# K and V of a fused linear-attention and SwiGLU kernel: plain products replaced by two-by-two block products with seven multiplications

## The chip, the cores and the metric

The kernel runs on one core of a Trainium2 chip. The metric is the device time of one execution in microseconds (us). The core has five engines with their own instruction streams: PE (TensorE, the matrix multiplier; its weight loads are listed as PEld), DVE (VectorE), ACT (ScalarE), POOL (GpSimd) and SP (SyncE, which only issues DMA transfers here). They meet through semaphores. Matmul results land in PSUM, eight banks of 128 x 512 fp32; everything else lives in SBUF.

## The reference

```python
xn = _layernorm(x)                       # x: 1 x 2048 x 1024, bf16
# attention block, 32 heads of 32
q, k, v = split(xn @ wqkv)               # wqkv: 1024 x 3072
phi = lambda t: where(t > 0, t + 1, exp(t)) + 1e-6
kv  = einsum("bhsd,bhse->bhde", phi(k), v)
z   = einsum("bhsd->bhd", phi(k))
o   = (phi(q) @ kv) / (phi(q) . z + 1e-6)
s   = o @ wo
# gated feed-forward block
g   = silu((silu(xn @ w_gate) * (xn @ w_up)) @ w_down)   # 1024 -> 3584 -> 1024
out = x + s * g
```

The attention is linear: `kv` and `z` sum over all 2048 tokens before any query is used. So K and V of all tokens come first.

## The kernel before

**Stages.** The 2048 tokens are 16 tiles of 128. The first stage normalises each tile (`ln_tile`), transposes it so that features lie on partitions (`t_tile`), multiplies it with the K and V columns of `wqkv` (`p_piece`), and adds its contribution to `kv` and `z` (`a_tile`). Then, for each half of the tokens (p = 0, 1), the kernel computes Q, gate and up in pairs of weight blocks, normalises Q by the denominators, and runs the down projection together with the attention output (`d_set`), which is joined with `kv` and `wo` into one matrix.

**K and V, lines 530 to 550.** Per tile there are four pieces (c = 0, 1 are K, c = 2, 3 are V), each eight matmuls of 128 x 128 by 128 x 512 into one PSUM bank. `phi_evac` (line 509) takes a K piece out: an exp on ACT, a minimum-and-add on DVE (L515), and a maximum-and-add on DVE (L516) that reads the bank again. A V piece is copied by ACT into `vext`, which has a column of ones per group for `z`. `a_tile` is eight matmuls of 129 columns into three banks (`kvb`) that stay open for the whole stage.

**Layer norm, lines 457 to 471.** DVE computes two `bn_stats` (L462, L463), an aggregate (L464) and variance plus epsilon (L465); POOL raises it to the power -0.5 (L466); DVE subtracts the mean and multiplies (L470).

**Transposes, lines 482 to 495.** Tiles 0 to 3 are transposed by PE into bank 7 (`MISC`), which is kept out of the pool of seven banks, and copied out by ACT. Tiles 4 to 15 use DMA transposes on SP.

**Seven products.** The later stages already use a two-by-two block scheme with seven products instead of eight. Class `Set` (line 636) holds one such product of 128-token or 128-column blocks: `step(m)` issues product m, which is four matmuls. Products 1 and 2 add up in bank a; bank b starts as an ACT copy of product 1 and takes 6, 7 and 4; product 5 is copied by ACT to SBUF (`s5`); DVE adds `s5` to b after step 6 (into bank c, which takes product 3) and again after step 7. The core of it:

```python
elif m == 6:
    self.grp(6, self.b, False)
    self.c = balloc()
    tt([bank_r[self.b], self.s5.r], [bank_r[self.c]], ps[self.c][:, :], ps[self.b][:, :],
       self.s5.ap(F32), ALU.add)
elif m == 7:
    self.grp(7, self.b, False)
```

The products need sums of blocks of both operands. `combos` (line 424) makes T1 to T4 of the moving operand in four DVE instructions, of which T1 overwrites R01; the stationary operand gets four sums too (`wload`, line 697). `run_pair` runs two sets interleaved in the order `PAIRSEQ`, in which steps 6 and 7 of a set are two steps apart.

**What sets the order.** Nothing is issued in the order it is written. `Plan` records each operation with its reads and writes, gives it a deadline (`dl`) from PE's accumulated time, and places operations greedily by a model of each engine's cost (lines 87 to 164). PE may take any ready group among the next six that are not done (`WINDOW=6`); DVE, ACT, POOL and SP take the ready operation with the earliest deadline. DMA loads are held back until 12 us before their deadline (`LEAD`). Each engine then runs its list strictly in order. `urgent` moves a deadline ahead. Banks are handed out by `balloc` and `bfree`, first in, first out, in program order.

Of the kernel before, what the change touches and what calls it, by code (L numbers as in the profile page):

```python
# [14 lines left out]
KB = 1024  # L15
# [204 lines left out]
def build_kernel(nc, A_x, A_wqkv, A_wo, B_w_gate, B_w_up, B_w_down, out, WINDOW=6, NWARM=14, LEAD=12.0):  # L220
# [12 lines left out]
    with ExitStack() as es:  # L233
# [38 lines left out]
        rstd = sbt("rstd", [128, 4, 1], F32)  # L272
        neg_half = sbt("neg_half", [128, 1], F32)
# [9 lines left out]
        MISC = 7  # L283
        banks = deque(range(7))
# [117 lines left out]
        pk_ring = Ring(W, 44 * KB, 2 * KB, 2)  # L402
# [36 lines left out]
        WK0 = 36 * KB  # L439
        wkv_r = [H.reg(WK0 + c * 8 * KB, 8 * KB) for c in range(4)]  # L440
        wkv = [H.at(WK0 + c * 8 * KB, 8 * KB).rearrange("p (kt n) -> p kt n", n=512) for c in range(4)]
        wo_r = [H.reg(68 * KB + c * 8 * KB, 8 * KB) for c in range(2)]
        wo = [H.at(68 * KB + c * 8 * KB, 8 * KB).rearrange("p (g n) -> p g n", n=512) for c in range(2)]

        xslot = {}

        def x_load(i):
            s = x_ring.take()
            xslot[i] = s
            dma([], [s.r], s.ap(), xf[i * 128:(i + 1) * 128, :], dsem("x%d" % s.k), 256 * KB).urgent = 10.0  # L450

        def wkv_load(c):
            dma([], [wkv_r[c]], wkv[c], wqkv_v[:, :, 1024 + c * 512:1024 + (c + 1) * 512], dsem("wkv%d" % c), 1024 * KB)

        xnslot = {}

        def ln_tile(i):
            j = i % 4
            s = xslot[i]
            xa = s.ap()  # L460
            sA, sB, mvr, ver, rsr = named("sA", j), named("sB", j), named("mv", j), named("ve", j), named("rs", j)
            dve([s.r], [sA], lambda h: h.bn_stats(stats[:, j, 0, :], xa[:, 0:512]), 512)  # L462
            dve([s.r], [sB], lambda h: h.bn_stats(stats[:, j, 1, :], xa[:, 512:1024]), 512)  # L463
            dve([sA, sB], [mvr], lambda h: h.bn_aggr(mv[:, j, :], stats[:, j, :, :]), 60)  # L464
            dve([mvr], [ver], lambda h: h.tensor_scalar(veps[:, j, :], mv[:, j, 1:2], EPS_LN, None, ALU.add), 60)  # L465
            pool([ver, nh_r], [rsr], lambda h: h.tensor_tensor(rstd[:, j, :], veps[:, j, :], neg_half[:, :], ALU.pow), 0.56)  # L466
            o = xn_ring.take()
            xnslot[i] = o
            oa = o.ap(FP16)
            dve([s.r, mvr, rsr], [o.r], lambda h: h.tensor_scalar(  # L470
                oa, xa, mv[:, j, 0:1], rstd[:, j, :], ALU.subtract, ALU.mult), 1024, 2.6)

        def xt_dest(i):
            p, j, m = i // 8, (i // 4) % 2, i % 4
            ar = X if p == 0 else P
            return ar, j, m

        def xt_keys(i, k):
            ar, j, m = xt_dest(i)
            return named("xt", i, k)  # L480

        def t_tile(i):
            s = xnslot[i]
            xa = s.ap(FP16)
            ar, j, m = xt_dest(i)
            if i >= 4:
                dst = ar.at(j * 8 * KB, 8 * KB, FP16).rearrange("p (k t) -> p k t", t=512)[:, :, m * 128:(m + 1) * 128]
                PL.op("sp", [s.r], [xt_r(i)], lambda h: h.dma_start_transpose(dst, xa), 0.08, sem=dsem("tx%d" % (i % 2)),
                      nbytes=400 * KB)
                return  # L490
            pb = ps[MISC][:, :].bitcast(FP16).rearrange("p (k t) -> p k t", t=128)
            trs = [(pb[:, kt, :], xa[:, kt * 128:(kt + 1) * 128], ident[:, :]) for kt in range(KT)]
            pe_tr([s.r, ident_r], [bank_r[MISC]], trs)
            dst = ar.at(j * 8 * KB, 8 * KB, FP16).rearrange("p (k t) -> p k t", t=512)[:, :, m * 128:(m + 1) * 128]
            act([bank_r[MISC]], [xt_r(i)], dst, pb[:, :, :], ACT.Identity)

        def xt_r(i):
            ar, j, m = xt_dest(i)
            keys = []
            for kt in range(KT):  # L500
                o = j * 8 * KB + kt * 1024 + m * 256
                keys += ar.reg(o, 256).keys
            return Region(keys)

        def xt_ap(i, kt):
            ar, j, m = xt_dest(i)
            return ar.at(j * 8 * KB + kt * 1024 + m * 256, 256, FP16)

        def phi_evac(src, src_r, out_ap, out_r, kind="ps"):
            e = e_ring.take()  # L510
            ea = e.ap(FP16)
            act([src_r], [e.r], ea, src, ACT.Exp, kind)
            b = B_ring.take()
            ba = b.ap(FP16)
            dve([e.r], [b.r], lambda h: h.tensor_scalar(ba, ea, 1.0, EPS_PHI, ALU.min, ALU.add), 512, 2.6)  # L515
            dve([src_r, b.r], [out_r], lambda h: h.scalar_tensor_tensor(  # L516
                out_ap, src, 0.0, ba, ALU.max, ALU.add), 512)

        kvb = [balloc(), balloc(), balloc()]

        def kv_ap(g):
            return ps[kvb[g // 3]][:, (g % 3) * 129:(g % 3) * 129 + 129]

        vext = TM.at(18 * KB, 4160).rearrange("p (s g n) -> p s g n", s=2, n=130)
        vx_r = [TM.reg(18 * KB, 2080), TM.reg(18 * KB + 2080, 2080)]
        pkv = {}
        for s2 in range(2):
            pool([], [named("vx1", s2), vx_r[s2], pool_chain], lambda h, s2=s2: h.memset(vext[:, s2, :, 128:129], 1.0))

        def p_piece(i, c):  # L530
            b = balloc()
            mms = [(ps[b][:, :], xt_ap(i, kt), wkv[c][:, kt, :], kt == 0, kt == KT - 1) for kt in range(KT)]
            pe_mm([xt_r(i), wkv_r[c]], [bank_r[b]], mms)
            if c < 2:
                if c == 0:
                    pkv[i] = pk_ring.take()
                s = pkv[i].sub(c * 1024, 1024)
                phi_evac(ps[b][:, :], bank_r[b], s.ap(), s.r)
            else:
                hb = c - 2  # L540
                act([bank_r[b], vx_r[i % 2]], [named("vx", i % 2, hb)], vext[:, i % 2, 4 * hb:4 * hb + 4, 0:128],
                    ps[b][:, :].rearrange("p (g n) -> p g n", n=128), ACT.Identity)
            bfree(b)

        def a_tile(i):
            s2 = i % 2
            pk = pkv[i].ap()
            mms = [(kv_ap(g), pk[:, g * 128:(g + 1) * 128], vext[:, s2, g, 0:129], i == 0 and g % 3 == 0, i == NT - 1)
                   for g in range(NG)]
            pe_mm([pkv[i].r, named("vx", s2, 0), named("vx", s2, 1), named("vx1", s2), vx_r[s2]], [bank_r[b] for b in kvb], mms)  # L550

        x_load(0)
        wkv_load(0)
        x_load(1)
        wkv_load(1)
        x_load(2)
        wkv_load(2)
        wkv_load(3)
        x_load(3)
        ln_tile(0)  # L560
        t_tile(0)
        ln_tile(1)
        p_piece(0, 0)
        t_tile(1)
        p_piece(0, 1)
        p_piece(1, 0)
        x_load(4)
        ln_tile(2)
        p_piece(0, 2)
        p_piece(1, 1)  # L570
        t_tile(2)
        p_piece(0, 3)
        p_piece(1, 2)
        a_tile(0)
        ln_tile(3)
        x_load(5)
        p_piece(1, 3)
        for it in range(3, NT + 2):
            if it + 3 < NT:
                x_load(it + 3)  # L580
            if it + 1 < NT:
                ln_tile(it + 1)
            if it < NT:
                t_tile(it)
            if it <= NT:
                for c in range(4):
                    p_piece(it - 1, c)
                a_tile(it - 2)
            else:
                a_tile(it - 2)  # L590


        KVZ = H.at(32 * KB, 2 * KB, FP16).rearrange("p (g n) -> p g n", n=128)
        KVT = H.at(34 * KB, 2 * KB, FP16).rearrange("p (g n) -> p g n", n=128)
        KVZ_r, KVT_r = H.reg(32 * KB, 2 * KB), H.reg(34 * KB, 2 * KB)
        z_r, zi_r, Zb_r = named("z"), named("zi"), named("Zb")
        for q, kb in enumerate(kvb):
            n = 3 if q < 2 else 2
            src = ps[kb][:, 0:129 * n].rearrange("p (g n) -> p g n", n=129)[:, :, 128:129]
            dst = zc[:, 3 * q:3 * q + n].rearrange("p (g n) -> p g n", n=1)  # L600
            dve([bank_r[kb]], [z_r], lambda h, dst=dst, src=src: h.tensor_copy(dst, src), 8)  # L601
# [527 lines left out]
```

## Time and profile before

| what | value |
|---|---|
| median of 3 runs | 764.66 us (762.93 to 766.51) |
| the profiled execution | 765.06 us |
| its span, first to last instruction | 763.1 us |
| PE busy | 748.0 us, 98% |
| DVE busy | 517.6 us, 68% |
| ACT busy | 296.9 us, 39% |
| granted TensorE clock, mean | 0.997 |
| first K/V matmul starts | 10.40 us |
| last `a_tile` starts | 132.87 us |

A row of the profile's groups names a line, an engine, an operation, the tiles written and read, their shapes and the count; then busy time and the mean in ns of one; then the engine's idle time just before, and who ended it. Many operations pass through helpers, so matmuls have line 209, transposes by PE line 216, ACT line 322 and DVE's two-tensor operations line 329. Rows of the timeline have the start in us, the duration, and the group; a bracket holds idle time and its releaser.

### The profile page before, as it was taken

What the parts mean: (1) busy time and instruction counts of PE and PEld (TensorE: products, weight loads), DVE (VectorE), ACT (ScalarE), POOL (GpSimd) and SP (SyncE); (2) the same over time, 40 slices, a digit from 0 to 9 for tenths busy, and PEclk for the clock granted to TensorE, in tenths of its full rate; (3) what the DMA queues carried; (4) which work ended last, traced back from release to release, by engine and by line L of the source; (5) the groups of instructions that cost most, each with busy time, mean ns of one, the idle gap of its engine ahead of it and who ended that gap; (6) DMA issues with size and microseconds to landing.
All of it is one profiled execution on the core that took longest, in us unless ns stands there. A gap on an engine that the chain in (4) does not pass through costs nothing.

```text
span 763.1 us, 9351 instructions
## 1 busy us (share of the span) xinstructions
PE 748.0 (98%) x3595; PEld 338.8 (44%) x3610; DVE 517.6 (68%) x945; ACT 296.9 (39%) x497; POOL 11.9 (2%) x33
## 2 busy tenths in 40 slices
PE   6999999999999999999999999999999999999997
PEld 3444445443444444444444444344444444444443
DVE  4665623868798677785574868788877778565463
ACT  2333333554565334322322254636634333222231
POOL 2100000000000000000000000000000000000000
PEclk9999999999999999999999999999999999999999
DMA  9333314525385332543547554246732336337740
GB/s 298 70 74 70 70 27 111 166 70 151 101 243 163 106 90 77 150 139 97 148 108 187 137 120 130 56 110 169 221 107 60 111 92 191 103 92 164 189 108 28
DMA packets 166795, 93.53 MB, mean 123 GB/s; under 512 B 31328, under 2 KB 162656, under 8 KB 166752
## 3 DMA queue, kind: packets, MB, share of 16 engines
q1 hardware_dynamic: 166752, 92.95, 45.0%
q8 instruction: 28, 0.46, 0.3%
q14 instruction: 15, 0.12, 0.1%
HBM read 75.50 MB, written 10.62 MB: 113 GB/s over the span
## 4 chain that ended last, share of the span: by engine, by line
PE 95%; ACT 2%; DVE 1%; DMA 1%; issue 0%; SPq 0%
PE ps L209 95%; DMA H<-in_A_wqkv_dram 1%; ACT H L322 0%; PE ps L216 0%; ACT TM L322 0%; DVE TM L329 0%; ACT L322 0%; DVE W L329 0%; DVE ps L329 0%; ACT ps L322 0%; ACT X L322 0%; SPq L332 0%; DVE H L606 0%; DVE H L516 0%; DVE zc L601 0%
## 5 line engine op out<-in xcount | busy, mean ns | idle before, releaser
L209 PE MATMUL ps<-X,W 128*128 128x512 f16 x1504 | 346.5, 379 | 1.2 <-DVE ps L329 1.1
L322 ACT ACTIVATE TM<-ps 128x512 f32<-128x512 f32 (+2 forms) x300 | 177.3, 595 | 241.1 <-PE ps L209 232.9
L209 PEld LDWEIGHTS ps<-X,W 128*128 128x128 f16 (+1 forms) x1504 | 144.6, 98 | 176.0 <-DVE ps L329 2.5
L209 PE MATMUL ps<-H,W 128*128 128x512 f16 x672 | 150.6, 379 | 1.4 <-ACT TM L322 1.4
L329 DVE TENSOR_TENSOR W<-W 128x1024 f16<-128x1024 bf16 (+3 forms) x224 | 133.9, 628 | 4.7 <-PE ps L209 2.3
L209 PE MATMUL ps<-P,W 128*128 128x512 f16 x512 | 122.8, 379 | 0.0
L209 PEld LDWEIGHTS ps<-H,W 128*128 128x128 f16 (+1 forms) x672 | 65.5, 98 | 81.0 <-ACT TM L322 2.4
L329 DVE TENSOR_TENSOR ps<-ps,TM 128x512 f32<-128x512 f32 x80 | 55.8, 697 | 65.2 <-PE ps L209 65.1
L329 DVE TENSOR_TENSOR TM<-ps,TM 128x512 f32<-128x512 f32 (+1 forms) x84 | 56.7, 675 | 55.4 <-PE ps L209 52.6
L322 ACT ACTIVATE TM<-TM 128x512 f16<-128x512 f32 (+1 forms) x54 | 33.4, 620 | 127.5 <-DVE TM L329 126.5
L322 ACT ACTIVATE ps<-ps 128x512 f32<-128x512 f32 x80 | 47.0, 587 | 83.4 <-PE ps L209 83.3
L209 PEld LDWEIGHTS ps<-P,W 128*128 128x128 f16 (+1 forms) x512 | 49.3, 98 | 59.0
L329 DVE TENSOR_TENSOR H<-ps,TM 128x512 f16<-128x512 f32 x84 | 57.8, 690 | 12.8 <-PE ps L209 12.6
L209 PE MATMUL ps<-H,X 128*128 128x512 bf16 x250 | 57.3, 384 | 3.6 <-DMA H<-in_A_wqkv_dram 2.2
L209 PE MATMUL ps<-H,P 128*128 128x512 bf16 x249 | 55.9, 379 | 0.4
L515 DVE TENSOR_SCALAR TM<-TM 128x512 f16<-128x512 f16 x64 | 17.9, 290 | 55.9 <-ACT TM L322 55.0
L329 DVE TENSOR_TENSOR TM<-TM 128x512 f16<-128x512 f16 (+1 forms) x60 | 25.1, 420 | 29.5 <-DMA TM<-TM 18.2
L329 DVE TENSOR_TENSOR H<-H 128x1024 f16<-128x1024 f16 (+1 forms) x74 | 41.0, 570 | 0.4
L209 PEld LDWEIGHTS ps<-H,X 128*128 128x128 f16 x256 | 24.7, 98 | 32.0 <-issue 3.1
L209 PEld LDWEIGHTS ps<-H,P 128*128 128x128 f16 x256 | 24.6, 97 | 28.4
L329 DVE TENSOR_TENSOR W<-H 128x1024 f16<-128x1024 f16 x38 | 25.5, 685 | 0.8 <-PE ps L209 0.5
L516 DVE SCALAR_TENSOR_TENSOR W<-ps,TM 128x512 bf16<-128x512 f32 x32 | 22.0, 687 | 1.1 <-PE ps L209 0.3
(59 smaller groups left out, 275.2 us busy)
## 6 DMA issues: line engine op xcount, KB each, us to landing
W<-in_B_w_gate_dram SPq DMA_DIRECT2D x28, 512.0 KB, 3.9
W<-in_B_w_up_dram SPq DMA_DIRECT2D x28, 512.0 KB, 5.2
W<-in_B_w_down_dram SPq DMA_DIRECT2D x16, 896.0 KB, 6.6
W<-in_A_x_dram SPq DMA_DIRECT2D x16, 256.0 KB, 2.8
H<-in_A_wqkv_dram SPq DMA_DIRECT2D x4, 1024.0 KB, 10.3
W<-in_A_wqkv_dram SPq DMA_DIRECT2D x8, 512.0 KB, 5.1
H<-r_scratch SPq DMA_DIRECT2D x32, 128.0 KB, 4.1
q_scratch<-H SPq DMA_DIRECT2D x8, 512.0 KB, 4.4
```

The source lines that it names most:

```text
L209: last = h.matmul(o, l, r, start=st, stop=sp, skip_group_check=True)
L322: return PL.op("act", reads, writes, lambda h: h.activation(o, i, func, **kw), nel(o) / 1200.0 + (0.055 if src == "ps" else 0.095))
L329: return dve(reads, writes, lambda h: h.tensor_tensor(o, a, b, op), nel(o), 1.92 if fast else 0.96)
L515: dve([e.r], [b.r], lambda h: h.tensor_scalar(ba, ea, 1.0, EPS_PHI, ALU.min, ALU.add), 512, 2.6)
L516: dve([src_r, b.r], [out_r], lambda h: h.scalar_tensor_tensor(out_ap, src, 0.0, ba, ALU.max, ALU.add), 512)
```

## The change

**K and V as sets.** The first pair of tiles keeps the plain pieces, 64 matmuls. The other seven pairs (u = 1 to 7) each become two sets, one for K and one for V: the two tiles and the two halves of the features are the blocks of the stationary side, the halves of the features and of the 1024 K (or V) columns those of the moving side. The K and V weights get new places and eight loads of 512 KB instead of four of 1 MB, with explicit order, and `combos` is called once for K and once for V; T1 overwrites R01, so both first tiles' pieces with j = 1 come first. `x_sums` makes the four token sums per pair on DVE. Sets run one behind the other: step 6 of one, step 1 of the next, one `a_tile`, 7, 5, 3, 2, 4.

**Evacuation.** K goes through `phi_evac` as before. For V, three of four blocks are ACT copies, and the block (1, 1) is written by the DVE addition itself into `vext` (`direct`). `vext` has four slots instead of two, K's features four slots instead of two.

**Layer norm.** From tile 2 on, DVE computes minus mean times the reciprocal deviation (one small instruction), and ACT does the scaling with per-row scale and bias.

**Banks and transposes.** Bank 7 joins the pool, which now has eight. The PE transposes of tiles 0 to 3 alternate between two banks from the pool (`tb`), which are freed with `rearm` (four small matmuls that overwrite the bank); tile 0 is done in two halves, one copied out by ACT, one by DVE. `kvt` and the last `turn` take a bank from the pool.

```diff
+        def xt_half(i, k):
+            ar, j, m = xt_dest(i)
+            return ar.at(j * 8 * KB + k * 4 * KB, 4 * KB, FP16).rearrange("p (q t) -> p q t", t=512)[
+                :, :, m * 128:(m + 1) * 128]
...
-        banks = deque(range(7))
+        banks = deque(range(8))
...
-            dve([s.r, mvr, rsr], [o.r], lambda h: h.tensor_scalar(
-                oa, xa, mv[:, j, 0:1], rstd[:, j, :], ALU.subtract, ALU.mult), 1024, 2.6)
+            if i < 2:
+                dve([s.r, mvr, rsr], [o.r], lambda h: h.tensor_scalar(
+                    oa, xa, mv[:, j, 0:1], rstd[:, j, :], ALU.subtract, ALU.mult), 1024, 2.6)
+            else:
+                dve([mvr, rsr], [nmr], lambda h: h.scalar_tensor_tensor(
+                    nmean[:, j, :], mv[:, j, 0:1], -1.0, rstd[:, j, :], ALU.mult, ALU.mult), 60)
+                act([s.r, nmr, rsr], [o.r], oa, xa, ACT.Identity, "sb", bias=nmean[:, j, :], scale=rstd[:, j, :])
...
+            for q, halves in enumerate(((0, 4), (4, 4)) if i == 0 else ((0, 8),)):
+                k0, n = halves
+                b = tb[(i + q) % 2]
...
+        def x_sums(u):
+            c = xs_ring.take()
+            cv = c.ap(FP16).rearrange("p (m q t) -> p m q t", m=4, t=128)
+            cr = [c.sub(q * KB, KB).r for q in range(4)]
+            A = {(k, i): xt_half(2 * u + i, k) for k in range(2) for i in range(2)}
+            ra = [xt_r(2 * u), xt_r(2 * u + 1)]
+            tt(ra, [cr[0]], cv[:, 0], A[0, 1], A[1, 1], ALU.add, True)
+            tt(ra + [cr[0]], [cr[1]], cv[:, 1], cv[:, 0], A[0, 0], ALU.subtract, True)
+            tt(ra, [cr[2]], cv[:, 2], A[0, 0], A[0, 1], ALU.subtract, True)
+            tt(ra + [cr[1]], [cr[3]], cv[:, 3], A[1, 0], cv[:, 1], ALU.subtract, True)
...
+            def direct(i, j, b, s5):
+                t = 2 * u + i
+                tt([bank_r[b], s5.r, vx_r[t % 4]], [named("vx", t % 4, j)], v_dest(t, j),
+                   ps[b][:, :].rearrange("p (g n) -> p g n", n=128), s5.ap(F32).rearrange("p (g n) -> p g n", n=128),
+                   ALU.add)
...
+        for n, (fn, args) in enumerate(((x_load, (0,)), (x_load, (1,)), (wkv_load, (0, 1)), (wkv_load, (0, 0)),
+                                        (x_load, (2,)), (wkv_load, (1, 1)), (x_load, (3,)), (wkv_load, (1, 0)))):
+            k = len(PL.ops)
+            fn(*args)
+            for o in PL.ops[k:]:
+                o.urgent = 60.0 - 2 * n
...
+        def prepare(u):
+            if u >= NT // 2:
+                return
+            for i in (2 * u, 2 * u + 1):
+                if i + 2 < NT:
+                    x_load(i + 2)
+            for i in (2 * u, 2 * u + 1):
+                ln_tile(i)
+                t_tile(i)
+            stats_of[u] = x_sums(u)
...
+        kvs(0)
+        for m in (1, 5, 2):
+            sets[0].step(m)
+        for n in range(len(todo)):
+            cur = kvs(n)
+            if todo[n][1] == 0:
+                prepare(todo[n][0] + 1)
+            nxt = kvs(n + 1)
+            for m, k in ((6, 1), (7, 5), (3, 2), (4, 0)):
+                cur.step(m)
+                if nxt is not None and k:
+                    nxt.step(k)
+                if k == 1 and fill:
+                    fill.popleft()()
+            if todo[n][1] == 1:
+                while fill:
+                    fill.popleft()()
+                fill.extend((partial(a_tile, 2 * todo[n][0]), partial(a_tile, 2 * todo[n][0] + 1)))
```

## The prediction

> **What bounds the kernel now.** I read the busy shares first, then the windows, then the timeline of TensorE, then the groups by shape.
>
> ```profile
> PE 748.0 (98%) x3595; PEld 338.8 (44%) x3610; DVE 517.6 (68%) x945; ACT 296.9 (39%) x497; POOL 11.9 (2%) x33
> ```
>
> TensorE is busy for 98% of a span of 763.1 us. Busy time flatters a pipelined engine, so I check it against a rhythm. In the steady K/V stage the timeline shows one group of eight narrow matmuls (`a_tile`) per token tile:
>
> ```profile
> 65.16 0.63 PE L209 MATMUL ps<-TM,W 128*128 128x129 bf16 x8
> ...
> 65.63 7.07 PE L209 MATMUL ps<-H,X 128*128 128x512 bf16 x32
> ...
> 72.54 0.63 PE L209 MATMUL ps<-TM,W 128*128 128x129 bf16 x8
> ...
> 79.91 0.63 PE L209 MATMUL ps<-TM,W 128*128 128x129 bf16 x8
> ```
>
> The period is (79.91 - 65.16)/2 = 7.375 us. `a_tile` holds 0.47 of it (65.16 to 65.63), so a 512-column matmul costs 6.905/32 = 0.2158 us, with no gap. The stage is bound by the number of matmuls. The other engines have room there (columns: window, then busy us and count of PE, weight load, DVE, ACT, POOL; granted clock; DMA share; GB/s):
>
> ```profile
> 30.00:40.00 10.00, 9.95 (x58) 5.05 (x58) 6.92 (x19) 3.20 (x6) 2.27 (x4) 1.00 0.38 79
> 100.00:110.00 10.00, 9.95 (x58) 5.03 (x58) 2.40 (x5) 3.37 (x6) 0.00 (x0) 1.00 0.27 52
> 140.00:150.00 10.00, 10.00 (x56) 4.20 (x54) 9.61 (x24) 5.95 (x11) 0.00 (x0) 1.00 0.97 299
> ```
>
> The third line matters most. It is the first Q pair, which already runs seven-product sets with the same exp-based evacuation, and there DVE is 96% busy while PE loses nothing.
>
> The exception to "PE is full" is the opening:
>
> ```profile
> 7.62 0.62 PE L216 MATMUL ps<-ident,W 128*128 128x128 f16 x8 [1.62 <-DVE W L470]
> 10.40 2.92 PE L209 MATMUL ps<-H,X 128*128 128x512 bf16 x8 [2.15 <-DMA H<-in_A_wqkv_dram]
> 13.12 1.06 PE L216 MATMUL ps<-ident,W 128*128 128x128 f16 x8
> 15.29 1.90 PE L209 MATMUL ps<-H,X 128*128 128x512 bf16 x8 [1.12 <-ACT X L322]
> ```
>
> PE waits for the first weights until 10.40 and then 1.12 us for one PSUM-to-SBUF copy of a transpose.
>
> **1. Matmuls removed.** Before: 16 tiles x 4 pieces x 8 = 512. After: the first pair keeps 2 x 4 x 8 = 64; the other seven pairs take 2 sets x 7 products x 4 = 56 each, 392; together 456. That is 56 fewer x 0.2158 = **-12.1 us**, on the path that sets the end. Weight loads fall by the same 56 and are hidden.
>
> **2. Matmuls added.** `rearm` for the two transpose banks and in `kvt`: three times four 128-column matmuls. One such group takes 0.23 us start to start (136.80 to 137.03 in the timeline): **+0.7**.
>
> **3. DVE, per pair.** These are the rows I price by:
>
> ```profile
> L329 DVE TENSOR_TENSOR ps<-ps,TM 128x512 f32<-128x512 f32 x80 | 55.8, 697 | 65.2 <-PE ps L209 65.1
> L329 DVE TENSOR_TENSOR X<-X 128x2048 f16<-128x2048 f16 x12 | 14.6, 1220 | 1.1 <-PE ps L209 1.0
> L329 DVE TENSOR_TENSOR W<-W 128x512 f16<-128x512 f16 x32 | 12.1, 419 | 0.5 <-DMA W<-m_scratch 0.4
> L322 ACT ACTIVATE ps<-ps 128x512 f32<-128x512 f32 x80 | 47.0, 587 | 83.4 <-PE ps L209 83.3
> L322 ACT ACTIVATE H<-H,zc 128x512 bf16<-128x512 bf16 x32 | 20.9, 712 | 0.3 <-DMA H<-r_scratch 0.3
> ```
>
> Back to back, a 0.69 us instruction gives way after 0.60 (at 27.15 and 27.75 two statistics start). Layer norm of two tiles, without the scaling but with the new small product for minus mean: 2 x (2 x 0.60 + 0.23 + 0.2 + 0.2) = 3.6. Four exp evacuations: 4 x (0.25 + 0.60) = 3.4. Two additions in each of two sets: 4 x 0.60 = 2.4. Token sums, 4 x 0.36 = 1.45 (the 419 ns row, less overlap). Sum 10.9. PE needs 56 x 0.2158 + 2 x 0.47 = 13.0 per pair, so DVE is 83% full. It was 2 x 2.1 + 3.4 = 7.6 of 14.75, 52%. It is not the bound, but its turns are now 0.6 us grains in a tight rhythm.
>
> **4. ACT, per pair.** Four bank copies (2.4), four exps (2.4), three V evacuations (1.8), two scalings. A scaling of 1024 elements with two per-row operands has no row. From the 712 ns row (512 elements, one operand), plus 512 elements (1021 - 597 = 424 ns between the 1024- and 512-element PSUM copies), plus one operand more (712 - 628 = 84 ns, 628 being a copy from SBUF): 1.22 us, an estimate. Sum 9.0 of 13.0, 69%. Here a rule speaks against the edit: the Trainium skill, "ScalarE: Activation LUTs", Rules for kernel authors, gives additions and multiplications to VectorE, up to about three times faster. The row agrees on the price: 0.54 us on DVE against 1.22. By the rule the move loses 14 x 0.68 = 9.5 us. By the windows, ACT is idle for two thirds of this stage and DVE is what becomes scarce, so I charge 0. The new wait is for POOL's power and DVE's product; behind it on ACT stand exps and bank copies, for which PE's next step waits. POOL takes 0.55, and a tile's chain can run almost a pair ahead (two slots each for normalised tiles and sums), so I leave it in item 6. Without cover it would cost up to 1.2 us a tile. On SP the DMA transposes of tiles 4 to 15 now wait for ACT's scaling, and loads of x stand behind them; a load is issued two tiles ahead, so this stays hidden too. POOL gets two more small memsets (0.16 each, in the 2.3 us it idles before its first power): nothing.
>
> **5. The opening.** Two banks for transposes instead of one let tile 1's transposes run before 10.40, in the wait for weights. The 1.12 us wait goes, and so does the 1.06 at half clock: **-2.0**. The weights become eight 512 KB loads in the same queue. The four extra issues (about 0.43 us each on SP) fall where SP is held by the queue anyway. First weights: 1.5 MB ahead, as before, so I keep 10.4 (between 9.5 and 11). Tile 2 moves behind the second megabyte of weights, and tiles 2, 3 are needed only after four to eight pieces (1.73 each), so nothing waits for them at once. What is late next is DVE. From 10.4 to about 39 us it must do the first pair's exps 3.4, norm of tiles 2 to 5 7.2, eight weight combinations at 1.2 = 9.6, two pairs' sums 2.9, and the first sets' exps and additions 5.8: 28.9 us in 28.6. I charge **+2** (between 0, as at 140 to 150, and 5).
>
> **6. The pipeline on five banks.** Step 7 writes the bank that DVE reads after step 6. Between them lie one step of the other set (0.86) and an `a_tile` (0.47): 1.33 us. The loop needs 0.20 (a V piece ends at 65.16, ACT starts at 65.36) plus 0.66 (DVE start 170.11 to PE start 170.77, the same addition in the second Q pair) = 0.86. Slack 0.47, less than one DVE grain. A bank comes back after exp, minimum and add, 0.20 + 0.63 + 0.33 + 0.66 = 1.82, and is wanted three steps later, 2.59: slack 0.77. The planner may take the next ready PE group within six, which hides most slips. I charge 0.15 us a set x 14 = **+2** (between 0, by the Q-pair window, and 0.9 x 14 = 12, if every turn slips one grain and nothing can pass). The four 1.2 us combinations for the later stage (about 73 us now) fall into this stage too: **+0.5** (0 to 2).
>
> **7. Later stages.** Eight banks instead of seven: at most the 1.1 us of DVE and 1.4 of ACT waits that PE has there. The re-planned order may move an activation-table load (1.28). I take **-0.3** (-1.5 to +1.5).
>
> Sum: -12.1 + 0.7 - 2.0 + 2 + 2 + 0.5 - 0.3 = **-9.2**. The profiled execution took 765.06 (1.96 around its span); 765.06 - 9.2 = 755.9. The median shown is 0.4 lower, so I say **755.5**.
>
> **Rivals.**
> (a) The saving arrives whole: DVE's load is hidden as at 140 to 150. Then -12.1 + 0.7 - 2.0 - 0.3 = -13.7, **751**. For it: that window. Against it: there DVE was full for 10 us, here for 100.
> (b) DVE sets the pace through the opening and the first half of the stage. Items 5 and 6 cost 5 + 5: -3.2, **761.5**. For it: 28.9 in 28.6. Against it: 2.1 us of DVE slack per pair to recover.
> (c) Slower: step 7 waits in every set because DVE is always in another instruction. It decides at 12.1/14 = 0.86 us a set, one whole step. At 1.25 a set it is +17.5 - 12.1 + 0.7 = +6, **771**. Behind it stands the Trainium skill, "TensorE: Matmul & The Clock Gate", A second HAM failure mode: a kernel that cycles PSUM banks idled between groups often enough for the clock to fall and rise again. The row: clock 0.83 in the window 10 to 20, after a wait, and 1.00 at 140 to 150, where sets cycle through banks. With the rule, seven falls[...] would eat the gain; with the row there is none. I go by the row, as single waits here stay under a microsecond.
> That the products are not saved is excluded: their number follows from the loops.
>
> **Chances.** Main case 0.60 (its own range 752.5 to 759), (a) 0.20, (b) 0.12, (c) 0.08. 0.5% is about what these runs can tell from no change: below 760.8 is faster. The main case and (a) all lie there, and a third of (b): 0.83; same 0.09, from (b); slower 0.08. For 8 in 10 I cut (c) and the outer ends of (a) and (b): 750.5 to 762.5.
>
> **What would show it.** Right: about 456 wide K/V matmuls at 0.216; the last `a_tile` near 124 instead of 133.34; first piece near 10.4 with no wait for ACT behind it; PE waits for DVE of 2 to 5 us in total up to 125; clock 1.00 from 20 on. Wrong: DVE waits above 10 us there, a clock under 1 in the stage, or weights landing past 11.

## The result and the profile after

Three runs of the changed kernel gave a median of **752.82 us** (752.08 to 754.16) against 764.66: ratio 0.985, 95% interval 0.980 to 0.989. On another chip, side by side, it was 752.88 (4 runs) against 762.56 (10 runs): ratio 0.988, interval 0.986 to 0.989, or 9.7 us by the medians.

The baselines probably differ because executions of the kernel before do: of 40 later ones, the 29 with a mean clock of 0.998 or more took 762.2 to 763.2 us and the 11 at 0.997 or less 764.3 to 767.1, and the execution that the prediction was built on (765.06 us, clock 0.997, a stretch at half clock in its opening) is of the second kind.

The page of the changed kernel, its busy shares:

```profile
PE 737.5 (98%) x3553; PEld 333.6 (44%) x3566; DVE 545.1 (72%) x1010; ACT 322.2 (43%) x532; POOL 13.4 (2%) x35
```

PE lost 10.5 us of busy time, DVE gained 27.5, ACT 25.3. The share of PE is 98% as before: the matmuls went, and the kernel became shorter with them. The timeline of PE in the K/V stage shows the new rhythm (start, duration, group):

```profile
64.37 0.63 PE L209 MATMUL ps<-H,TM 128*128 128x129 bf16 x8
...
71.74 0.63 PE L209 MATMUL ps<-H,TM 128*128 128x129 bf16 x8
...
77.39 0.63 PE L209 MATMUL ps<-H,TM 128*128 128x129 bf16 x8
...
84.76 0.63 PE L209 MATMUL ps<-H,TM 128*128 128x129 bf16 x8
```

Every second `a_tile` is one pair of tiles later: 77.39 - 64.37 = 13.02 us, and 84.76 - 71.74 = 13.02. That is 56 x 0.2158 + 2 x 0.47 = 13.02, without any gap; it was 14.75. The windows say the same (columns as before the change: busy us and count of PE, weight load, DVE, ACT, POOL; clock; DMA share; GB/s):

```profile
20.00:30.00 10.00, 9.12 (x59) 4.50 (x58) 9.56 (x22) 6.48 (x9) 2.12 (x2) 1.00 0.16 56
30.00:40.00 10.00, 9.91 (x58) 4.95 (x57) 9.86 (x23) 8.01 (x12) 1.35 (x3) 1.00 0.51 106
60.00:70.00 10.00, 9.95 (x52) 4.75 (x52) 9.74 (x29) 6.67 (x11) 1.24 (x3) 1.00 0.41 93
100.00:110.00 10.00, 9.95 (x53) 4.80 (x53) 6.33 (x13) 5.77 (x10) 0.00 (x0) 1.00 0.39 105
```

From 30 us on PE is as full as before, while DVE is 97 to 99% busy in the second and third line (69% and 56% before). DVE is full for some 50 us and PE waits for nothing. Of the four lines, only the first shows a loss.

The pairs alone do not fill DVE in that stretch. From 30 to 80 us PE gets through 50/13.02 = 3.84 pairs, about 42 us of DVE by item 3's 10.9, an estimate. The rest is work for later: DVE takes the statistics of ten tiles, where 3.84 pairs use up 7.7, two weight combinations left over from the opening, and two for the later stage. The last tile's norm is done at about 82 us, and from 90 to 100 us DVE is only 61% busy. The groups have the new costs:

```profile
L329 DVE TENSOR_TENSOR ps<-ps,TM 128x512 f32<-128x512 f32 x94 | 65.6, 698 | 66.6 <-PE ps L209 66.2
...
L329 DVE TENSOR_TENSOR H<-H 128x2048 f16<-128x2048 bf16 x8 | 9.7, 1214 | 2.7 <-PE ps L209 1.9 <-DMA H<-in_A_wqkv_dram 0.8
...
L322 ACT ACTIVATE W<-W,nmean,rstd 128x1024 f16<-128x1024 bf16 x14 | 17.3, 1238 | 2.2 <-DVE nmean L559 2.2
```

The first is the addition of product 5 (80 of them before, 14 more now), the second the eight weight combinations, the third the scaling on ACT: 1.238 us, where the estimate was 1.22.

The opening, PE's timeline of the changed kernel:

```profile
7.37 0.64 PE L216 MATMUL ps<-ident,W 128*128 128x128 f16 x8
9.51 1.89 PE L209 MATMUL ps<-H,X 128*128 128x512 bf16 x8 [1.50 <-DMA H<-in_A_wqkv_dram]
11.23 0.61 PE L216 MATMUL ps<-ident,W 128*128 128x128 f16 x8
13.00 5.35 PE L209 MATMUL ps<-H,X 128*128 128x512 bf16 x23 [1.16 <-ACT X L322]
18.54 1.90 PE L209 MATMUL ps<-H,X 128*128 128x512 bf16 x8 [0.19 <-DVE TM L617]
...
23.52 2.76 PE L209 MATMUL ps<-H,X 128*128 128x512 bf16 x11 [0.47 <-ACT H L322]
26.61 0.62 PE L216 MATMUL ps<-ident,W 128*128 128x128 f16 x8 [0.33 <-ACT W L322]
```

Tile 1's transposes (11.23) still stand behind the first piece, and the wait for ACT's copy is still there, 1.16 us. The first piece starts at 9.51 and runs at full clock (1.89 for eight matmuls, 2.92 in the profiled execution of before). Three new short waits have come, at 18.54, 23.52 and 26.61. What the last one hangs on is told by the chain of waits of this execution (start, length, what; "issue" is time that nothing in the profile explains):

```profile
14.94 1.23 DVE H L329
16.16 0.60 DVE stats L547
...
21.09 0.59 DVE stats L548
...
22.39 1.09 DVE H L329
...
23.62 1.47 POOL rstd L551
...
25.11 0.17 DVE nmean L559
...
25.31 1.25 ACT W L322
26.61 0.62 PE ps L216 x8
```

From 14.94 to 26.61 the path runs almost only over DVE, POOL and ACT: combinations of weights, statistics of tiles 2 and 3, the power, the small product, the scaling. In the kernel before, the same stretch of the chain is PE.

### The profile page after: what moved, and what is told of

Read it like the earlier page. It is cut to its first block, busy times and chain, and to the rows that moved or that the text cites. A ratio compares the mean times of both kernels' runs of the same rounds, so it can differ in the third digit from the quotient of the medians.

```text
span 752.4 us, 9403 instructions
## 1 busy us (share of the span) xinstructions
PE 737.5 (98%) x3553; PEld 333.6 (44%) x3566; DVE 545.1 (72%) x1010; ACT 322.2 (43%) x532; POOL 13.4 (2%) x35
## 4 chain that ended last, share of the span: by engine, by line
PE 90%; DMA 3%; DVE 3%; ACT 2%; issue 1%; SPq 0%; POOL 0%; DVEq 0%
PE ps L209 90%; DMA W<-in_B_w_up_dram 1%; DMA W<-m_scratch 1%; DMA H<-in_A_wqkv_dram 1%; DVE H L329 1%; ACT TM L322 1%; ACT H L322 1%; SPq L332 0%; DVE W L329 0%; DVE TM L329 0%; ACT L322 0%; PE ps L216 0%; ACT W L322 0%; DVE ps L329 0%; POOL rstd L551 0%
## 5 line engine op out<-in xcount | busy, mean ns | idle before, releaser
L322 ACT ACTIVATE TM<-ps 128x512 f32<-128x512 f32 (+1 forms) x275 | 161.6, 595 | 177.2 <-PE ps L209 172.8
L209 PE MATMUL ps<-H,W 128*128 128x512 f16 (+1 forms) x891 | 203.4, 379 | 0.3
L209 PEld LDWEIGHTS ps<-H,W 128*128 128x128 f16 (+1 forms) x896 | 87.2, 98 | 103.6 <-DVE ps L329 0.2
L329 DVE TENSOR_TENSOR H<-ps,TM 128x512 f16<-128x512 f32 (+1 forms) x91 | 62.5, 690 | 14.2 <-PE ps L209 14.0
L329 DVE TENSOR_TENSOR H<-H 128x1024 f16<-128x1024 f16 (+2 forms) x82 | 50.8, 634 | 3.1 <-PE ps L209 1.9
L209 PE MATMUL ps<-H,X 128*128 128x512 bf16 (+1 forms) x133 | 32.2, 379 | 3.5 <-DMA H<-in_A_wqkv_dram 1.5
L322 ACT ACTIVATE H<-ps 128x512 bf16<-128x512 f32 (+2 forms) x42 | 24.2, 615 | 10.3 <-PE ps L209 10.3
L209 PE MATMUL ps<-H,P 128*128 128x512 bf16 (+1 forms) x93 | 22.8, 379 | 0.2
L209 PE MATMUL ps<-W 128*128 128x512 f16 x76 | 21.8, 379 | 0.0
L322 ACT ACTIVATE H<-H,zc 128x512 bf16<-128x512 bf16 x32 | 20.9, 712 | 0.4 <-DMA H<-r_scratch 0.4
```

The lines of the kernel that those rows point to most:

```text
L209: last = h.matmul(o, l, r, start=st, stop=sp, skip_group_check=True)
L322: return PL.op("act", reads, writes, lambda h: h.activation(o, i, func, **kw), nel(o) / 1200.0 + (0.055 if src == "ps" else 0.095))
L329: return dve(reads, writes, lambda h: h.tensor_tensor(o, a, b, op), nel(o), 1.92 if fast else 0.96)
```

## The experiments

Where a number "against the changed kernel" is given, it is against 752.88, its median beside the kernel before. The variants ran on three chips, where the kernel before had medians of 762.63 (V with plain pieces up to the scaling on DVE), 762.56 (the changed kernel again, tile 1's transposes, the longer warm-up) and 762.94 (the others), so a few tenths of a microsecond between them mean nothing. All diffs but the last are against the changed kernel.

**The theory.** The stage takes the whole saving because PE's order leaves enough slack between a step and the DVE work that it waits for; what is lost is lost mostly in the opening, to a chain over DVE, POOL and ACT. Rivals: V's half of the sets is worth less than its matmuls; DVE costs time all through the stage; step 7's wait is close to deciding; moving the scaling to ACT was a loss, as the rule cited in item 4 has it.

**V with plain pieces, K in sets.** Interleaved as p_piece and step; V's four weight combinations are not needed.

```diff
-        combos(KVV[1])
...
+            st.step(1)
+            p_piece(2 * u, 1, 1)
+            st.step(5)
+            st.step(2)
+            fill.popleft()()
+            p_piece(2 * u + 1, 1, 1)
+            st.step(6)
+            p_piece(2 * u, 1, 0)
+            st.step(7)
...
```

> One part alone: K in sets, V in plain pieces (four per pair, put between the steps of the K set), and no combinations of V's weights. 28 matmuls more than the changed kernel. If TensorE's count sets the time: +28 x 0.2158 = +6.0 us against the changed kernel (752.8), so about 758.8, less up to 1.7 for a lighter opening. If DVE's turns set it (V's sets put 4.8 us of combinations and 14 x 0.6 us of additions on DVE), most of the 6.0 comes back: 752 to 755.

Measured: 756.84 (756.65 to 757.38), ratio 0.992 [0.990, 0.994] to the kernel before. V's sets are worth 4.0 us, where their 28 matmuls come to 6.0. The windows of PE and DVE:

```profile
20.00:30.00 10.00, 9.53 (x61) 4.88 (x59) 8.29 (x24) 6.95 (x10) 2.01 (x3) 1.00 0.18 55
30.00:40.00 10.00, 10.00 (x60) 5.02 (x58) 7.63 (x23) 7.30 (x11) 1.06 (x2) 1.00 0.72 150
```

With less DVE work (8.29 instead of 9.56 in the first line) PE is busier in the opening (9.53 instead of 9.12), and the wait for the scaling ahead of tile 3's transposes is not there. That wait was 0.33 us (0.5 in full, as explained below the table in the next section), so this part of V's missing 2 us is lost in the opening. Where the rest goes is not shown.

**Three of four matmuls in every K and V product.** A quarter of each product is left out, so the result is not the reference's; what DVE, ACT and the banks do is unchanged. If PE alone sets the stage, 14 x 7 x 0.2158 = 21.1 us go.

```diff
-                return 4, [([(ws[q], xa[:, q, :]) for q in range(4)], [wr, xr])]
+                return 3, [([(ws[q], xa[:, q, :]) for q in range(3)], [wr, xr])]
```

> Every K/V product of a set uses three of its four matmuls (one quarter of each product is left out), everything else stays. TensorE loses 14 x 7 x 0.2158 = 21.1 us of work. If TensorE alone bounds the stage, the time falls by all of it, to about 731.7. If DVE is just behind (10.9 us a pair by the prediction's sum), a pair can't go under 10.9 while TensorE would need 10.0, so at most 7 x 2.1 = 15 us come, to 738 or more, with TensorE waiting for DVE.

Measured: 736.66 (736.14 to 738.94), 16.2 less than the changed kernel: 4.9 of the 21.1 do not arrive. Two windows:

```profile
40.00:50.00 10.00, 8.98 (x49) 4.16 (x47) 9.83 (x25) 8.00 (x13) 1.09 (x2) 1.00 0.41 102
80.00:90.00 10.00, 9.70 (x58) 4.72 (x56) 9.95 (x22) 8.14 (x13) 0.84 (x1) 1.00 0.41 89
```

Now PE waits for DVE. The timeline of PE shows how, from one `a_tile` to the same one a pair later:

```profile
77.70 0.63 PE L209 MATMUL ps<-H,TM 128*128 128x129 bf16 x8
...
83.64 1.47 PE L209 MATMUL ps<-H,W 128*128 128x512 f16 x6 [0.30 <-DVE ps L329]
...
88.18 0.63 PE L209 MATMUL ps<-H,TM 128*128 128x129 bf16 x8
```

A pair needs 42 x 0.2158 + 0.94 = 10.0 us of PE and takes 88.18 - 77.70 = 10.48, with one wait, for the addition of product 5; the next pair takes 10.48 again. The rest of the missing 4.9 us is lost before, while norms and the last weight combinations are still on DVE's list. DVE is the next bound, about 2.5 us a pair behind PE. (10.48 is not the price that item 3 summed: from 77.70 on DVE has hardly any norm left to do and makes combinations for the later stage instead.)

**A second read of bank b by DVE after step 6.** Another 0.69 us addition, into a spare place, between step 6 and step 7, in each of the 14 sets. If step 7 were near its limit, this would show.

```diff
...
+                    if self.twice:
+                        tt([bank_r[self.b], self.s5.r], [TM.reg(13 * KB, KB)], TM.at(13 * KB, KB, FP16), ps[self.b][:, :],
+                           self.s5.ap(F32), ALU.add)
...
+            st.twice = True
```

> After step 6 of each K/V set DVE adds bank b and the saved product 5 a second time, into scratch that nobody reads; step 7 has to wait for both reads. Nothing else changes. If turns decide (rival c): the loop from 6 to 7 needs 0.86 + 0.60 = 1.46 of 1.33 us, and each set loses from 0.13 (1.8 us in all) up to a whole DVE grain of 0.6 (8.4 us in all). If the planner can pass other groups ahead and DVE still has room (12.1 of 13.0 us a pair): 0 to 1 us.

Measured: 753.03 (752.23 to 754.32), the time of the changed kernel. Two windows, and the one wait for DVE that PE's timeline shows after 30 us in the stage:

```profile
50.00:60.00 10.00, 10.00 (x60) 5.05 (x58) 9.71 (x26) 6.08 (x9) 1.10 (x2) 1.00 0.47 100
80.00:90.00 10.00, 10.00 (x54) 4.77 (x52) 9.73 (x22) 6.43 (x10) 2.19 (x2) 1.00 0.15 29
```

```profile
65.28 1.90 PE L209 MATMUL ps<-H,W 128*128 128x512 bf16 x8 [0.24 <-DVE ps L329]
```

The work is there (14 additions of 0.68 us; DVE 9.73 at 80 to 90, where it was 7.70), and it costs next to nothing: PE is 10.00 in both windows, and one wait of 0.24 us is all that comes up inside the stage. (Around the last `a_tile`, a wait for ACT grows from 0.22 to 0.69 us and the next one for DVE shrinks from 0.93 to 0.29.) The order of PE groups was planned anew around it. Rival (c), a wait of 0.86 us or more a set, is far off.

**The scaling back on DVE in all tiles.**

```diff
-            if i < 2:
+            if i < 16:
```

> The scaling of layer norm goes back from ACT to DVE for all tiles, all else as in the changed kernel. DVE has 0.54 - 0.15 = 0.39 us more a tile (5.5 us in all), ACT 1.24 less (17.3 in all). If DVE is what is scarce: up to +5.5 us. If DVE still has room (11.7 of 13.0 a pair): within 1 us of the changed kernel. If ACT's slower scaling cost time on the way[...]: faster than the changed kernel, by up to 9.8 us.

Measured: 754.08 (753.53 to 754.79), 1.2 more than the changed kernel. The ranges overlap (the changed kernel's goes from 752.19 to 755.23), but the profiles agree: from the first piece to the last `a_tile` it is 114.3 us here and 112.6 in both profiles of the changed kernel. PE's timeline has a wait that the changed kernel doesn't have, for one of DVE's token sums:

```profile
29.45 1.04 PE L209 MATMUL ps<-H,W 128*128 128x512 f16 x4 [0.68 <-DVE W L329]
```

Four shorter waits for DVE or ACT follow inside the stage (0.17 to 0.33). DVE needs 0.54 us for a scaling and ACT 1.24, yet ACT is the better place here: DVE is full from 20 to 80 us, and ACT is not. The gain is 1 to 2 us, however, not the 14 x 0.39 = 5.5 that DVE is spared (0.54 less the small product's 0.15): most of that was covered.

**Tile 1's transposes ahead of the first piece** (what item 5 assumed), by a dependency of the first piece on them; and the same with the first transpose bank freed as soon as tile 2 is through.

```diff
-        p_piece(0, 0, 1)
         t_tile(1)
+        t1 = [o for o in PL.ops if o.eng == "pe"][-1]
+        p_piece(0, 0, 1, t1)
...
+        rearm(tb[0])
```

> The transposes of tile 1 are put ahead of the first K piece, into the wait for the first weights, which the prediction took for granted and the changed kernel did not do. If that step of the prediction was only mis-scheduled: 0.45 for the transposes and 1.16 for the wait for ACT go, -1.6 us against the changed kernel. If DVE's list (combinations, statistics) is what the opening waits for in the end, its waits further on grow by as much: 0 to -0.5.

> As the run before, and the first transpose bank is given back right after tile 2's transposes in program order instead of after all pieces but one, so that the last pieces and the first set find a fourth bank. If the 0.47 us wait for ACT at 23.5 us is a wait for a bank: another -0.5 us. If it is covered by DVE's lateness: 0.

Measured: 752.67 (752.29 to 753.08) and 752.75 (752.32 to 753.23) beside 752.88 for the changed kernel in the same series: no gain. The first one's timeline of PE:

```profile
8.66 0.62 PE L216 MATMUL ps<-ident,W 128*128 128x128 f16 x8 [0.52 <-DVE X L589]
9.12 8.82 PE L209 MATMUL ps<-H,X 128*128 128x512 bf16 x39
19.39 0.62 PE L216 MATMUL ps<-ident,W 128*128 128x128 f16 x8 [1.44 <-ACT W L322]
...
26.11 0.62 PE L216 MATMUL ps<-ident,W 128*128 128x128 f16 x8 [0.92 <-ACT W L322]
```

The 1.16 us wait for ACT is gone, as item 5 had it. But PE only arrives earlier at the transposes of tiles 2 and 3, and waits there for the scaling, 1.44 and 0.92 instead of 0 and 0.33. With the bank freed early the 0.47 wait goes as well, and the wait at tile 3 becomes 1.56. So the 0.47 was a wait for a bank, and the end of the opening hangs on the chain shown above. Both versions also lengthen that chain: tile 2's power on POOL, 0.55 us in the changed kernel, now falls beside a weight combination of DVE and takes 1.46 (see the last section; the first version's row):

```profile
16.40 1.46 POOL L551 TENSOR_TENSOR rstd<-veps,neg_half 128x1 f32<-128x1 f32 x1 [8.86 <-DVE veps L550]
```

Time that PE gains ahead of this chain is given back at its end.

> The changed kernel itself, beside the next three on one chip, as their measure. Expected 752.8, within 0.3%.

That is the changed kernel in the same series, 752.88.

**The opening in another order.** Transposes first as above; tiles 2 and 3 of x loaded behind the first megabyte of weights, their norms ahead of the weight combinations, their scaling on DVE. A second version loads all of x ahead of the weights.

```diff
-            if i < 2:
+            if i < 4:
...
-                o.urgent = 60.0 - 2 * n
+                o.urgent = (560.0, 558.0, 550.0, 60.0, 58.0, 50.0, 48.0, 46.0)[n]
...
-        ln_tile(2)
+        pushed(ln_tile, 2, 40.0)
```

> The opening written anew, all else as in the changed kernel: tile 1's transposes ahead of the first piece; tiles 2 and 3 of x loaded right behind the first megabyte of weights; their norms ahead of the weight combinations in DVE's list, scaled by DVE. If the opening of the changed kernel waits for DVE's list (combinations, then the norm of tile 3 with a POOL power of 1.47 us and an ACT scaling of 1.24): the 1.6 us that tile 1's transposes alone did not bring and the waits of about 1 us at 17 to 26 us come back, -2 to -2.5 us against the changed kernel (752.9), near 750.5. POOL's power takes 0.55 again where no combination runs beside it. If the weights' arrival bounds the opening instead, the 0.5 MB of x ahead of the second megabyte costs up to 1.4 us and the gain is 0 to -1.

> The same new opening, but all four tiles of x are loaded ahead of any weights. If bytes ahead of the first weights set the first piece's start: 0.5 MB at 0.35 MB/us, +1.4 us against the run before this one, less what DVE gains by having the norms done. If DVE's list sets it: within 0.5 us of the run before this one.

Measured: 752.16 (751.39 to 753.04) and 752.21 (750.74 to 753.94), on a chip where the kernel before took 762.94: 0.7 below the changed kernel's median in the other series, within the spread of both. The 2 to 2.5 us that were expected did not come. From the first one, PE's timeline and then two windows:

```profile
14.89 0.62 PE L216 MATMUL ps<-ident,W 128*128 128x128 f16 x8 [2.09 <-DVE W L556]
```

```profile
10.00:20.00 10.00, 7.86 (x51) 4.07 (x51) 9.89 (x20) 4.22 (x7) 2.10 (x2) 1.00 1.08 357
20.00:30.00 10.00, 9.95 (x50) 4.64 (x50) 9.56 (x21) 4.69 (x9) 0.96 (x2) 1.00 0.04 14
```

PE is now full from 20 to 30 us, but it lost the time from 10 to 20, where DVE is 99% busy: here the order moved the wait. The second version, its first pieces and the same first window:

```profile
10.56 5.19 PE L209 MATMUL ps<-H,X 128*128 128x512 bf16 x16
```

```profile
10.00:20.00 10.00, 9.95 (x57) 5.09 (x59) 7.34 (x14) 4.65 (x6) 0.96 (x2) 0.83 1.08 354
```

Behind its first piece PE waits for nothing until the last `a_tile`: with the statistics of the first four tiles ahead of the combinations, and their scaling on DVE, the waits of the opening are gone. It pays with weights that land 1.37 us later than in the first version (10.56 against 9.19; +1.4 was expected) and, in this execution, with a stretch at half clock (5.19 us for 16 matmuls that take 3.62 in the first version). Only one of its five executions had a mean clock of 1.0. It took 750.74 us, 1.3 less than any of the seven of the changed kernel; one execution is too little to call this order faster.

**The opening of the kernel before.** Twice as many warm-up matmuls, to see what its half clock costs; and the unchanged kernel again, for a second profile.

```diff
-...WINDOW=6, NWARM=14, LEAD=12.0):
+...WINDOW=6, NWARM=28, LEAD=12.0):
```

> The kernel before, with 28 instead of 14 warm-up matmuls, and nothing else. It splits the gain of the opening into clock and schedule. If the half-speed stretch from 11 to 15 us in the kernel before came from the idle TensorE ahead of it: the first piece takes 1.9 instead of 2.9 us and the transposes 0.6 instead of 1.06, -1.5 us against the kernel before, unless the warm-up itself delays the first transposes (14 more at 0.216 = 3.0 us, ending near 9, with the first transposes due at 7.6: up to +1 back). If the clock follows something else: 0 to +1.

> The kernel before, to see a second opening of it. The profile shown of it took 765.06, while its median beside the changed kernel was 762.56. If the difference is the half-speed clock of the first piece (1.03 + 0.45 us) and later weights (about 0.8): a profile near 762.5 shows the first piece starting near 9.6 and taking 1.9 us.

Measured: 764.88 (764.64 to 765.33) with the longer warm-up, 2.3 more than its neighbour before (762.56) and outside all that was expected; the piece ran at full clock but started at 11.49, behind the warm-up. So it says what a longer warm-up costs and not what the half clock costs. The unchanged kernel: 762.83 (762.39 to 765.72), and its profiled execution took 762.39, with a span of 760.4. Its timeline of PE:

```profile
9.13 1.90 PE L209 MATMUL ps<-H,X 128*128 128x512 bf16 x8 [1.12 <-ACT X L322]
10.87 0.61 PE L216 MATMUL ps<-ident,W 128*128 128x128 f16 x8
12.64 1.90 PE L209 MATMUL ps<-H,X 128*128 128x512 bf16 x8 [1.16 <-ACT X L322]
...
130.21 0.63 PE L209 MATMUL ps<-TM,W 128*128 128x129 bf16 x8
```

Weights at 9.13 at the latest, full clock, and the last `a_tile` 2.66 us sooner than in the profile that the prediction had (132.87). The late weights and the half clock belonged to that execution, not to every one of the kernel.

## Why the prediction was right, and where it was not

The time was in the range and on the right side. It lies at the low edge of the likeliest case's own range (752.5 to 759), and nearer to rival (a)'s 751 than to its 755.5. I predicted -9.2, and the medians side by side give -9.7. Step by step, the two profiles of like openings (before_again, span 760.4; after_again, span 750.5):

| step | predicted | measured | from |
|---|---|---|---|
| 1 matmuls | -12.1 | -12.1 | 7 pairs, 14.75 us each, then 13.02 |
| 2 rearm | +0.7 | +0.7 | three times 0.23 |
| 5 start | -2.0 | -0.3 | first piece 9.13, then 8.85 |
| 5 DVE late | +2.0 | +1.5 | three waits up to 26 us: 0.36 + 0.63 + 0.50 |
| 6 pipeline | +2.5 | +0.4 to +0.8 | one wait of 0.38 ahead of the last `a_tile`; 0.4 in no visible place |
| 7 later stages | -0.3 | -0.5 | what follows the last `a_tile`, 630.2, then 629.1 |
| sum | -9.2 | -9.9 | spans 760.4, then 750.5 |

That the sum came out so well is in part luck: the start missed by 1.7 us and the pipeline by about 2, in opposite directions. The start in the table also varies by some tenths from one profile to the next (8.7 to 9.6).

In the waits, each bracket has some 0.17 us added, the modelled tail of the matmul before it. For step 7, four Q matmuls (0.86) that now run ahead of the last `a_tile`, and one `rearm` (0.23), are taken out.

**Item 1** was right: the rhythm without gaps is shown by the timeline. **Item 3** was right that DVE is not the bound of the stage: in three_of_four, where PE does wait for it, a pair takes 10.48 us. Its sum of 10.9 was not measured as such, but its prices hold: statistics start 0.60 us apart (16.08 and 16.68 in the changed kernel), token sums 0.34 (29.64 and 29.98).

**Item 4** was right that the move is no loss, and right on the price (1.238). The Trainium skill's rule in "ScalarE: Activation LUTs", Rules for kernel authors, would have made it 9.5 us slower; norm_on_dve shows 1.2 us the other way. The rule weighs one instruction against another; here the engine that it recommends was full. In the opening, though, item 4's chain is not covered: POOL's power, put at 0.55, takes 1.47 there, and ACT's scaling stands behind it.

**Item 5** failed in its mechanism. "Two banks for transposes instead of one let tile 1's transposes run before 10.40" did not happen: they run behind the first piece, and the 1.16 us wait is there. And had it happened, it would have brought nothing, as t1_first shows: the end of the opening is set by the chain over DVE, POOL and ACT. Of the -2.0, the 1.06 at half clock was read from one execution and is not the kernel's; the 1.12 us wait is (1.16 in the second profile of before), but it stayed. "First weights: 1.5 MB ahead, as before, so I keep 10.4" was wrong with it: 8.7 to 9.6 in the profiles of the changed kernel and of those variants that load in its order. The second half, "what is late next is DVE", was near in place and size, 1.5 against 2, but not for its reason. It set 28.9 us of work against 28.6; in the profile DVE is idle for 3.4 of the 10 us from 10 to 20, waiting for PE's first pieces and ACT's copies. What is late is the chain that ends in tile 3's norm, with POOL's power (1.47) and ACT's scaling (1.25) at its end.

**Item 6** was too dear. In the profile no turn of the stage waits before the last `a_tile`: step 7's slack of 0.47 us was "less than one DVE grain", and yet double_read adds a grain in every set for one wait of 0.24 us. That the planner's choice among six PE groups makes this slack is likely: one `a_tile` is written per set, 6.51 us apart, and they run 7.37 and 5.65 apart. But no run had a smaller `WINDOW`, so it is not shown. Inside the stage rival (a) was right; what rival (b) feared came in the opening only, 1.5 us instead of 5. (c) and its failure of the clock did not come: the clock is 1.00 in every window from 20 us on.

That the forecast time was 2.7 us above the measured one comes from the base. The sum started at 765.06, the execution with the late weights and the half clock; from the 762.39 of the second profile it gives 753.2. In the same way the last `a_tile` came at 122.09 instead of near 124.

## What to carry to other kernels

An engine that is 95% busy is no bound as long as each of its results has slack; part of what fills it may not be due yet. What shows a bound is the consumer's waits, not the busy share. Where a chain of work must be through before the first loop can turn, as in an opening, adding up one engine's work is not enough: follow the chain over all engines, and expect a gain elsewhere to come back as a wait at its end, unless the chain itself becomes shorter. Before pricing a wait in an opening, take a second execution: late weights and a stretch at half clock were worth 2 to 3 us here and were not the kernel's.

## What the runs showed of the hardware

**POOL beside DVE.** POOL's power on 128 values usually takes 0.55 us. Where it starts while DVE runs a weight combination (two 16-bit operands in SBUF, 1.22 us), it takes 1.46. The changed kernel's timeline of POOL, and then of DVE:

```profile
17.97 0.55 POOL L551 TENSOR_TENSOR rstd<-veps,neg_half 128x1 f32<-128x1 f32 x1 [10.77 <-DVE veps L550]
23.62 1.46 POOL L551 TENSOR_TENSOR rstd<-veps,neg_half 128x1 f32<-128x1 f32 x1 [5.10 <-DVE veps L550]
```

```profile
17.80 1.28 DVE L617 SCALAR_TENSOR_TENSOR TM<-ps,TM 128x512 bf16<-128x512 f32 x2
...
23.46 1.22 DVE L329 TENSOR_TENSOR H<-H 128x2048 f16<-128x2048 bf16 x1
```

The second power ends at 25.08, 0.40 us after the combination (24.68), and the two like it in t1_first also end 0.40 after theirs: it looks as if the power could begin only then. The first runs beside operations with one operand in PSUM and isn't held up. The Trainium skill, "SBUF — State Buffer", Who interferes with whom, describes a port pair that a DVE instruction with two SBUF operands and a GpSimd instruction that reads SBUF can't hold at once; the rows agree. The 0.9 us lies on the chain of the opening; a version that changes only this was not tried.

**The clock in the opening.** PE idles between its warm-up and its first piece in every profile, and only some of them fall to half clock: not with 1.50 us of idle time in the changed kernel's profile, but with 2.15 in the first profile of before, and with 1.48 in that of three_of_four, where the first eight matmuls took 3.49 us. What decides it was not found.
